# Lending dead SBUF as exponential buffers in a four-layer attention kernel, with fewer passes over the keys in its first layer

## The chip, the cores and the metric

The kernel runs as one launch on one core of a Trainium2 chip. The metric is the device time of the launch in microseconds; the profile is of one execution, and its times count from the first instruction.

## The reference

One sequence x of 2048 rows and 512 columns (bf16) goes through four layers with a residual each: A, B, A, B. Both A layers use the same weights, and so do both B layers.

```python
# A: 32 query heads of 16, one key and one value head for all of them
q = (x @ wq) as 32 heads;  k = x @ wk;  v = x @ wv
p = softmax(q k^T / 4)                  # 32 x 2048 x 2048
y = (p v) joined over the heads @ wo
# B: linear attention, 32 heads of 16
q, k, v = split(x @ wqkv);  phi(t) = where(t > 0, t + 1, exp(t)) + 1e-6
kv = sum_s phi(k)^T v;  z = sum_s phi(k)
y = (phi(q) kv / (phi(q) z + 1e-6)) joined @ wo
# each layer: x = x + layer(layernorm(x))
```

## The kernel before

**A planner writes the order.** The Python code does not emit instructions directly. It runs a small event simulation (class `Planner`): each operation (`op`) has a duration per engine, a latency, reads, writes and a priority; generators (`process`) wait for flags, for operations, or for a buffer from a pool (`acq`). The order in which the simulated engines take operations is written out per engine, with semaphore waits for the dependences. On the chip each engine runs its list in that fixed order, so durations in the code decide only the order. Operations that may run on ACT or DVE (`flex`, `copy_flex`) get the engine that is free first in the simulation.

**Softmax layers (L = 0 and 2, `run_a`).** x has 16 tiles of 128 rows. For a tile t the 32 heads are computed as two halves (`par`), each with four groups j of heads at four 32-row positions of PE. A *score block* is 128 keys x 512 (4 heads x 128 queries): 2 x 16 x 2 x 4 = 2048 blocks per layer, 4096 in all (`KM` and `QT`, L838). A *segment* (`Seg`) is one (t, par) with a range of key tiles `kts`; segments are computed in the order of `a_segs`. With all keys at once a tile has one segment per half. Early tiles run before all keys exist, in passes over ranges of keys:

```python
PASSES = ((0, 2), (2, 4))
LATE = ((4, 8), (8, 12), (12, 16))
```

The first four tiles take all of these, so that they have five segments each (tiles 2 and 3 have four).

**Two engines compute the exponentials.** Scores go to two sets of three PSUM banks. ACT takes a set's first two or all three banks with one exact exponential (L1006) into one of `NPT` = 6 buffers `PT`. Where DVE has time, it takes the third bank, or another free one (`dve_split`, `dve_open`, `alone`): it builds the exponential's bits with one addition and a maximum, written as int16 into a quarter of one of `NFB` = 12 buffers `FB` (L1085). Four such blocks make a chunk, and the chunk is copied three times with a fixed number added (a *shift*, L1127, `dve_shifts`); PE then multiplies all four versions with differently weighted values (`VW`), which smooths the error of the bit trick. So a block on ACT needs one product with V (L892, PT), a block on DVE four (L892, FB). Where PE has a gap, a filler matmul that adds zero is issued to keep its clock up (L937 in the softmax layers, L824 elsewhere).

**Sums.** A segment's products accumulate in one PSUM bank (`ACC`). At its end DVE copies the bank into a fp32 sum in `sacc` (L1150, first segment of a tile half) or adds it there (L1152). After the last one the sum is transposed, normalised and projected (`norm`, `epilogue`) and x is updated.

**Linear layers (L = 1 and 3, `run_b`)** are computed tile by tile as x tiles come out of the softmax layer before, in the gaps of the exponentials; phi uses one ACT activation (L1254) per 128x512. Their keys are accumulated over all tiles, so that the outputs of layer 1 wait for the last tile of layer 0; layer 2 starts as its x tiles come. Layer norm (`ln_tile`) writes `xn`, one of six buffers, and its transpose goes to `xnT` (512 x 2048, all 16 tiles), by a DMA transpose issued from SP or by PE.

**What starts the exponentials.** `act_stream` waits for the keys of tiles 0 and 1 and the first Q. Before a block is taken, all keys of its segment must be planned. DVE's exponentials start when the last key group is planned (`KGATE`). Thresholds for DVE's share: `BLS`, `BLT`, `BLO`, `DXB` (DVE's backlog in us up to which it takes a block), `FBO`, `FBS` (free FB buffers to keep), `AHEAD`, `CHT`, `ENDL` (how far ahead of ACT).

**Memory that is dead for a while.** `OB` and `OTB` (buffers of layer 1's output) are used by layer 1 alone; `wq` only while Q is computed; `wo2` (the weight of B) only at the end of each B layer; `xn` buffers little once the keys are done; `sacc` rows of early tiles after those tiles' end; and most of `xnT` after the queries of layer 2 are computed.

Of the kernel before, what the change touches and what calls it, by code (L numbers as in the profile page):

```python
# [6 lines left out]
BF16 = mybir.dt.bfloat16  # L7
# [28 lines left out]
class Planner:  # L36
# [39 lines left out]
    def op(self, opts, reads=(), writes=(), prio=5.0, lat=0.08, dma=False, name="", join=None, mode="full", port=False, after=()):  # L76
# [13 lines left out]
        for k in list(writes) + list(after):  # L90
            deps.update(self.ws(k))
            deps.update(self.readers.get(k, ()))
# [301 lines left out]
PASSES = ((0, 2), (2, 4))  # L394
LATE = ((4, 8), (8, 12), (12, 16))
# [22 lines left out]
PBL = 1.2  # L418


def bass_interleave_layers__grouped_kv_mqa__linear_attn_block__prompt_kernel(
# [66 lines left out]
    OB = sb("OB", [P, NOB, D], BF16)  # L488
    OTB = sb("OTB", [P, NOB, 4, P], BF16)
# [22 lines left out]
    def give(pool, item):  # L512
        if pool is banks and retire.get(item):
# [8 lines left out]
    pl.give = give  # L522

# [12 lines left out]
    def dma(dst, src, writes, prio, lat):  # L536
        return op({SP: (0.07, lambda e: e.dma_start(dst, src))}, writes=writes, prio=prio, lat=lat, dma=True)

    for t in range(4):
        dma(x_sb[:, t, :], xv[:, t, :], [("x", t)], 0.1 * t, 2.5 + 0.5 * t)  # L540
    dma(wk[:], A_wk.rearrange("(ft f) c -> f ft c", f=P), ["wk"], 1.0, 4.0)
    dma(wv[:], A_wv.rearrange("(ft f) c -> f ft c", f=P), ["wv"], 1.1, 4.2)
    dma(wq[:], A_wq.rearrange("(ft f) c -> f ft c", f=P), ["wq"], 1.2, 5.5)
    for b in range(1, 4):
        dma(x_sb[:, 4 * b:4 * b + 4, :], xv[:, 4 * b:4 * b + 4, :], [("x", t) for t in range(4 * b, 4 * b + 4)], 2.0 + 0.1 * b, 6.0 + 1.5 * b)
    def late():
# [3 lines left out]
        dma(wo2[:], B_wo.rearrange("(g r) c -> r g c", r=P), ["wo2"], 3.2, 16.0)  # L550
# [45 lines left out]
    def flex(fn_a, fn_d, da, dd, reads, writes, prio, aprio=None):  # L596
        return op({AC: (da, fn_a), DV: (dd, fn_d)}, reads=reads, writes=writes, prio=prio)

    def copy_flex(dst, src, reads, writes, prio, da=0.5, dd=0.62):
        return flex(lambda e: e.copy(dst, src), lambda e: e.tensor_copy(dst, src), da, dd, reads, writes, prio)  # L600
# [10 lines left out]
    xn_pool = Pool_(range(NXN))  # L611

    def dmat(dst, src, reads, writes, prio):
        return op({SP: (0.1, lambda e: e.dma_start(dst, src, transpose=True))}, reads=reads, writes=writes, prio=prio, lat=DTL, dma=True)
# [5 lines left out]
    def halves(bs, dst, key, prio, psrc=None):  # L620
        l = op({DV: (DH_DUR, lambda e: e.tensor_copy(dst(0), psrc(bs[0], 0)))}, writes=[B_(bs[0]), key], prio=prio)
        r = op({AC: (AH_DUR, lambda e: e.copy(dst(1), psrc(bs[1], 1)))}, writes=[B_(bs[1]), key], prio=prio, join=l)
# [53 lines left out]
    def ln_tile(t, prio, far=False, crit=False):  # L676
# [3 lines left out]
        else:  # L680
# [10 lines left out]
           reads=[("x", t), ("mv", t), ("rs", t)], writes=[("xn", i)], prio=prio, port=True)  # L691
        if far:
            o = dmat(xnT[:, :, t * P:(t + 1) * P], xn[:, i, :], [("xn", i)], [("xnT", t)], prio)
# [3 lines left out]
        if crit:  # L697
# [3 lines left out]
            halves(bs, lambda h: xnT[:, 2 * h:2 * h + 2, t * P:(t + 1) * P], ("xnT", t), prio, lambda b, h: bank_bf(b)[:, 0:2, :])  # L701
# [12 lines left out]
        c = copy_flex(xnT[:, :, t * P:(t + 1) * P], v, [], [B_(b), ("xnT", t)], prio, 0.48, 0.34)  # L714
        pl.give_after(banks, b, [c])


    def a_tile(L, t, prio):
# [5 lines left out]
        yield from ln_tile(t, prio, t >= FARA[L // 2], cr)  # L724
# [67 lines left out]
    def a_segs():  # L792
        segs = []
        done = 0
        for lo, hi in PASSES:
            for t in range(hi):
                kts = list(range(lo, hi)) if t < lo else list(range(hi))
                for par in range(2):
                    segs.append(Seg(len(segs), t, par, kts, t >= lo, False, 2 * t + par))
            done = hi  # L800
        for lo, hi in LATE:
            for t in range(done):
                for par in range(2):
                    segs.append(Seg(len(segs), t, par, list(range(lo, hi)), False, hi == T, 2 * t + par))
        for t in range(done, T):
            for par in range(2):
                segs.append(Seg(len(segs), t, par, list(range(T)), True, True, 0))
        return segs

    pt_pool = Pool_(range(NPT))  # L810
    fb_pool = Pool_(range(NFB))
# [17 lines left out]
    def run_a(L):  # L829
        segs = a_segs()  # L830
# [113 lines left out]
        def act_stream():  # L944
            yield ("flag", ("K", L, 0))
            yield ("flag", ("K", L, 1))
# [5 lines left out]
            while True:  # L952
# [3 lines left out]
                while len(group) < size[s_] and split is None and state["si"] < len(segs):  # L956
                    sg = segs[state["si"]]
                    if not sg.left:
                        state["si"] += 1
                        continue  # L960
# [6 lines left out]
                    while any(("K", L, kt) not in pl.flags for kt in sg.kts) or ("Q", L, sg.t) not in pl.flags:  # L967
# [725 lines left out]
```

## Time and profile before

| what | value |
|---|---|
| median of 3 runs | 1533.74 us |
| lowest, highest | 1529.07, 1533.83 us |
| span of the profiled execution | 1530.0 us (no other time is given for it) |
| first to last exponential of ACT, layer 0 | 13.41 to 730.53 us |
| step from layer 0's to layer 2's exponentials | 730.53 to 754.79 us |
| first to last exponential of ACT, layer 2 | 754.79 to 1492.30 us |
| tail | 1492.30 to 1530.00 us |
| busy: PE, DVE, ACT, POOL | 94%, 94%, 97%, 4% of the span |

A row of a group reads: line, engine, operation, output tile <- input tiles, shapes, count | busy time in us, mean ns of one | idle time of the engine just before them, and what ended it. Busy time counts overlapping instructions once; the mean is of each by itself, so the mean times the count can be more. A row of the busy table reads: stretch, its length, busy us of PE, PEld, DVE, ACT, POOL with instruction counts, the granted PE clock as a share of full speed, the DMA share and GB/s. A row of a timeline reads: start, length, engine, line, operation, output <- input, count, and in brackets idle time before it. Equal neighbours in a timeline are merged into one row with their count.

### The profile page before, as it was taken

What the parts mean: (1) busy time and instruction counts of PE and PEld (TensorE: products, weight loads), DVE (VectorE), ACT (ScalarE), POOL (GpSimd) and SP (SyncE); (2) the same over time, 40 slices, a digit from 0 to 9 for tenths busy, and PEclk for the clock granted to TensorE, in tenths of its full rate; (3) what the DMA queues carried; (4) which work ended last, traced back from release to release, by engine and by line L of the source; (5) the groups of instructions that cost most, each with busy time, mean ns of one, the idle gap of its engine ahead of it and who ended that gap; (6) DMA issues with size and microseconds to landing.
All of it is one profiled execution on the core that took longest, in us unless ns stands there. A gap on an engine that the chain in (4) does not pass through costs nothing.

```text
span 1530.0 us, 35778 instructions
## 1 busy us (share of the span) xinstructions
PE 1440.2 (94%) x14498; PEld 522.9 (34%) x14606; DVE 1440.2 (94%) x2702; ACT 1482.6 (97%) x1503; POOL 63.8 (4%) x126
## 2 busy tenths in 40 slices
PE   8999999999999999999999989999999999999998
PEld 4422222333332223333644323323333332333335
DVE  7999999999999999999767899999999999999996
ACT  7999999999999999999699999999999999999996
POOL 4000000000000000000011000000000000000001
PEclk8999999999999999999999999999999999999999
DMA  4100010000000000000000000100000000000001
GB/s 112 70 2 1 9 22 5 8 7 6 8 8 8 5 8 5 1 1 2 2 1 1 2 1 9 22 5 9 9 5 8 9 8 5 8 5 1 1 2 56
DMA packets 40434, 17.53 MB, mean 11 GB/s; under 512 B 34128, under 2 KB 39760, under 8 KB 40272
## 3 DMA queue, kind: packets, MB, share of 16 engines
q1 hardware_dynamic: 40272, 15.25, 4.3%
q8 instruction: 117, 1.92, 0.5%
q14 instruction: 45, 0.37, 0.1%
HBM read 5.28 MB, written 2.10 MB: 5 GB/s over the span
## 4 chain that ended last, share of the span: by engine, by line
PE 29%; DVE 25%; issue 22%; ACT 22%; POOL 1%; DMA 0%; SPq 0%; ACTq 0%; POOLq 0%
ACT PT L1006 21%; DVE FB L1085 12%; PE ps L892 11%; DVE FB L1127 9%; PE ps L838 8%; PE ps L606 3%; PE ps L763 2%; PE ps L937 2%; PE ps L1169 1%; DVE sacc L1150 1%; ACT phE L1254 1%; DVE sacc L1152 0%; DVE Osb L1180 0%; PE ps L824 0%; POOL rs L686 0%
## 5 line engine op out<-in xcount | busy, mean ns | idle before, releaser
L1006 ACT ACTIVATE PT<-ps 128x1024 bf16<-128x1024 f32 (+1 forms) x1342 | 1418.1, 1204 | 14.8 <-PE ps L838 7.4
L1085 DVE TENSOR_SCALAR FB<-ps 128x512 int16<-128x512 f32 x1022 | 672.7, 682 | 19.0 <-PE ps L838 17.0
L838 PE MATMUL ps<-QT,KM 32*128 32x512 bf16 x4096 | 543.9, 386 | 43.1 <-ACT PT L1006 29.2
L892 PE MATMUL ps<-FB,VW 128*32 128x512 bf16 x4088 | 537.8, 385 | 20.1 <-ACT PT L1006 10.3
L892 PE MATMUL ps<-PT,V 128*32 128x512 bf16 x3074 | 523.7, 387 | 7.1 <-ACT PT L1006 5.4
L1127 DVE TENSOR_SCALAR FB<-FB 128x2048 int16<-128x2048 int16 (+1 forms) x768 | 503.1, 678 | 1.0
L838 PEld LDWEIGHTS ps<-QT,KM 32*128 32x128 bf16 x4096 | 136.4, 91 | 437.4 <-ACT PT L1006 295.4
L892 PEld LDWEIGHTS ps<-FB,VW 128*32 128x32 bf16 x4088 | 136.2, 94 | 217.7 <-issue 110.2
L892 PEld LDWEIGHTS ps<-PT,V 128*32 128x32 bf16 x3074 | 128.5, 94 | 112.9 <-issue 61.5
L937 PE MATMUL ps<-QT,V 128*32 128x512 bf16 (+6 forms) x579 | 139.8, 315 | 0.9 <-DVE FB L1085 0.3
L686 POOL TENSOR_TENSOR rs<-ve,mhalf 128x1 f32<-128x1 f32 x64 | 43.4, 680 | 1394.9 <-DVE ve L684 1392.3
L606 PE MATMUL ps<-wqkv,xnT 128*128 128x512 bf16 (+1 forms) x212 | 66.5, 369 | 3.4 <-issue 2.1
L937 PEld LDWEIGHTS ps<-QT,V 128*32 128x32 bf16 x579 | 46.1, 95 | 62.8 <-issue 43.6
L1150 DVE COPY sacc<-ps 128x512 f32<-128x512 f32 x64 | 43.6, 681 | 10.1 <-PE ps L892 9.9
L1254 ACT ACTIVATE phE<-ps 128x512 bf16<-128x512 f32 (+1 forms) x66 | 41.4, 628 | 7.6 <-PE ps L763 6.2
L1169 PE MATMUL ps<-identF,sacc 128*128 128x128 f32 x256 | 46.0, 291 | 0.9 <-DVE sacc L1150 0.8
L682 DVE BATCH_NORM_STATS2 st<-x_sb 128x6 f32<-128x512 bf16 x60 | 40.7, 680 | 2.5 <-DMA x_sb<-in_A_x_dram 2.3
L1152 DVE TENSOR_TENSOR sacc<-sacc,ps 128x512 f32<-128x512 f32 x56 | 38.0, 678 | 1.8 <-PE ps L892 1.7
L763 PE MATMUL ps<-xnT,wqkv 128*128 128x128 bf16 x512 | 39.4, 220 | 0.1
L763 PE MATMUL ps<-xnT,wq 128*128 128x128 bf16 x480 | 38.6, 226 | 0.0
L606 PEld LDWEIGHTS ps<-wqkv,xnT 128*128 128x128 bf16 x272 | 22.1, 97 | 46.5 <-issue 34.6
L1169 PEld LDWEIGHTS ps<-identF,sacc 128*128 128x128 f32 x256 | 27.4, 140 | 20.7 <-issue 11.5
(142 smaller groups left out, 656.5 us busy)
## 6 DMA issues: line engine op xcount, KB each, us to landing
out_dram<-x_sb SPq DMA_DIRECT2D x16, 128.0 KB, 1.7
x_sb<-in_A_x_dram SPq DMA_DIRECT2D x3, 512.0 KB, 6.1
wqkv<-in_B_wqkv_dram SPq DMA_DIRECT2D x1, 1536.0 KB, 7.4
xnT<-xn SPq DMA_TRANSPOSE x36, 2.4
x_sb<-in_A_x_dram SPq DMA_DIRECT2D x4, 128.0 KB, 2.5
wq<-in_A_wq_dram SPq DMA_DIRECT2D x1, 512.0 KB, 4.2
wo<-in_A_wo_dram SPq DMA_DIRECT2D x1, 512.0 KB, 4.1
wo<-in_B_wo_dram SPq DMA_DIRECT2D x1, 512.0 KB, 8.3
```

The costliest lines, as they stand in the source:

```text
L606: return e.matmul(dst, lhsT=l, rhs=r, start=(k == 0), stop=(k == len(pairs) - 1))
L686: op({PO: (0.55, lambda e: e.tensor_tensor(out=rs[:, t:t + 1], in0=ve[:, t:t + 1], in1=mhalf[:], op=ALU.pow))}, reads=[("ve", t), "mhalf"] ...
L763: ins = e.matmul(dst[:, g * P:(g + 1) * P], lhsT=lhs(g, k), rhs=rhs(k), start=(k == 0), stop=(k == FT - 1))
L838: return e.matmul(bank(b), lhsT=KM[r, sg.par, kt * P:(kt + 1) * P], rhs=QT[r, sg.t, :], start=True, stop=True)
L892: ins = e.matmul(ps[32 * j:32 * j + 32, ACC * 512:(ACC + 1) * 512], lhsT=V[:, kt, :] if w is None else VW[:, kt, w, :], rhs=ap, start=(k = ...
L937: o = op({PE: (n / 2400.0, lambda e: e.matmul(ps[32 * j:32 * j + 32, b * 512:b * 512 + n], lhsT=V0[:], rhs=QT[:, sg.t, 0:n], start=st, sto ...
L1006: ex = op({AC: (0.051 + 0.4267 * n, lambda e, n=n, s_=s_, p_=p_: e.activation(PT[:, p_, 0:n * 512], ps[:, s_ * 512:(s_ + n) * 512], ACTF.E ...
L1085: o = op({DV: (0.602, lambda e: e.tensor_scalar(out=dst.bitcast(I16), in0=bank(b), scalar1=VB, scalar2=VLO, op0=ALU.add, op1=ALU.max))}, w ...
L1127: o = op({en: (du, lambda e, w=w, g_=g_: e.tensor_scalar(out=FB[:, g_, 0:n].bitcast(I16), in0=FB[:, f_, 0:n].bitcast(I16), scalar1=float(w ...
L1150: o = op({DV: (0.6, lambda e, src=src: e.tensor_copy(src, bank(ACC)))}, writes=[B_(ACC), key], prio=0.0, lat=0.15)
L1169: o = op({PE: (0.12, lambda e, c=c: e.transpose(ps[:, b * 512 + c * P:b * 512 + (c + 1) * P], src[:, c * P:(c + 1) * P], identF[:]))}, rea ...
L1254: op({AC: (0.07 + n / 1200.0, lambda e: e.activation(phE[:, i, 0:n], bank(b, n), ACTF.Exp))}, reads=[B_(b)], writes=[("phE", i)], prio=pr ...
```

## The change

Line numbers in the text are those of the kernel before.

- Layer 0's early tiles: two instead of four, with key ranges 0-2, 2-4 and 4-16. Layer 2: as before up to key tile 8, then 8-16 in one pass.
- In layer 0 the exponentials start with the first key tile, and a block waits only for its own key tile, not for all of its segment.
- Lent buffers ("guests"): two PT and two FB in the joined OB/OTB memory, four PT in xnT columns of tiles 4 to 15 (layer 2), one FB each in two rows of `sacc`, in four `xn` buffers, in `wq` and in `wo2`. `lend` puts a guest into its pool when its owner ("host") is done; `recall` takes it back near the end of the layer. The first write of a guest, and the first write of the host after it, get the dependences of the other (`behind`). FB buffers can so rise from 12 to as many as 18, PT from 6 to 8 in layer 0 and 10 in layer 2.
- `wq` is loaded a second time after layer 0, `wo2` after layer 0 (no longer at the start) and again after layer 2. Layer 3 uses only the first four tiles of xnT, in a ring.
- The planner's durations and latencies of loads are replaced by measured ones.
- Thresholds are set per softmax layer (`TUNE`).

```diff
-PASSES = ((0, 2), (2, 4))
-LATE = ((4, 8), (8, 12), (12, 16))
+SEQ = {0: ((2, 0, 2), (2, 2, 4), (2, 4, 16)), 2: ((2, 0, 2), (2, 2, 4), (4, 0, 4), (4, 4, 8), (4, 8, 16))}
...
+BACK = 2
+TUNE = {0: {"FBS": 5, "AHEAD": 15, "LAG": 0.15, "ENDL": 12, "FBO": 0, "BLO": 7.0, "DXB": 1.6, "BLT": 3.2},
+        2: {"FBS": 3, "DXB": 1.6, "ENDL": 9, "BLS": 1.0}}
...
-    OB = sb("OB", [P, NOB, D], BF16)
-    OTB = sb("OTB", [P, NOB, 4, P], BF16)
+    OBB = sb("OBB", [P, 2 * NOB, D], BF16)
+    OB = OBB[:, 0:NOB, :]
+    OTB = OBB[:, NOB:2 * NOB, :].rearrange("p n (g c) -> p n g c", c=P)
...
+    for i in range(2):
+        pts[NPT + i] = OBF[:, i * BUF:(i + 1) * BUF]
+        home["PT", NPT + i] = ob_keys
+        fbs[NFB + i] = OBF[:, i * 2048:(i + 1) * 2048]
+        home["FB", NFB + i] = ob_keys
+    for i in range(4):
+        pts[NPT + 2 + i] = xnT[:, i, 4 * P:S]
+        home["PT", NPT + 2 + i] = xt_keys
...
+    def recall(which):
+        for kind, i in which:
+            if (kind, i) not in lent:
+                continue
+            lent.discard((kind, i))
+            pool = pt_pool if kind == "PT" else fb_pool
+            if i in pool.free:
+                pool.free.remove(i)
+                returned(pool, i)
...
-    dma(wq[:], A_wq.rearrange("(ft f) c -> f ft c", f=P), ["wq"], 1.2, 5.5)
+    load_wq()
...
-        dma(wo2[:], B_wo.rearrange("(g r) c -> r g c", r=P), ["wo2"], 3.2, 16.0)
...
+    def ring(L, t):
+        return t % 4 if L == 3 else t
...
             yield ("flag", ("K", L, 0))
-            yield ("flag", ("K", L, 1))
+            globals().update(TUNE[L])
+            if L:
+                yield ("flag", ("K", L, 1))
...
-                    while any(("K", L, kt) not in pl.flags for kt in sg.kts) or ("Q", L, sg.t) not in pl.flags:
+                    while any(("K", L, kt) not in pl.flags for kt in (sg.kts if L else blk[:1])) or ("Q", L, sg.t) not in pl.flags:
...
-                ex = op({AC: (0.051 + 0.4267 * n, lambda e, n=n, s_=s_, p_=p_: e.activation(PT[:, p_, 0:n * 512], ps[:, s_ * 512:(s_ + n) * 512], ACTF.Exp, scale=EXPSC, bias=EXPBIAS))},
-                        writes=bk + [("PT", p_)], prio=1.0, lat=EX_LAT)
+                ex = op({AC: (0.051 + 0.4267 * n, lambda e, n=n, s_=s_, p_=p_: e.activation(pts[p_][:, 0:n * 512], ps[:, s_ * 512:(s_ + n) * 512], ACTF.Exp, scale=EXPSC, bias=EXPBIAS))},
+                        writes=bk + [("PT", p_)], prio=1.0, lat=EX_LAT, behind=guest(L, "PT", p_))
...
+        def spare():
+            if L == 0:
+                for i in range(2):
+                    lend(pt_pool, "PT", NPT + i)
+            yield ("flag", ("K", L, T - 1))
+            hold_xn()
+            if L == 0:
+                lend(fb_pool, "FB", NFB + 5)
+                for t in range(T):
+                    yield ("flag", ("Q", L, t))
+                lend(fb_pool, "FB", NFB + 4)
+                return
+            for t in range(T):
+                yield ("flag", ("x", 1, t))
+            lend(fb_pool, "FB", NFB + 5)
+            for i in range(2):
+                lend(fb_pool, "FB", NFB + i)
+            for t in range(T):
+                yield ("flag", ("Q", L, t))
+            lend(fb_pool, "FB", NFB + 4)
+            for i in range(4):
+                lend(pt_pool, "PT", NPT + 2 + i)
```

More of the change, by code (lines that the diff above doesn't have):

```diff
@@ L74, in ws, with op @@
         return self.writer.get(k, [])
-    def op(self, opts, reads=(), writes=(), prio=5.0, lat=0.08, dma=False, name="", join=None, mode="full", port=False, after=()):
+    def op(self, opts, reads=(), writes=(), prio=5.0, lat=0.08, dma=False, name="", join=None, mode="full", port=False, after=(), behind=()):
         o = Op()
@@ L89, in op @@
             deps.update(self.ws(k))
-        for k in list(writes) + list(after):
+        for k in list(writes) + list(after) + list(behind):
             deps.update(self.ws(k))
@@ L522, in bass_interleave_layers__grouped_kv_mqa__linear_attn_block__prompt_kernel, with lend, hold_xn, returned @@
     pl.give = give
+    pt_pool = Pool_(range(NPT))
+    fb_pool = Pool_(range(NFB))
+    xn_pool = Pool_(range(NXN))
+    xheld = {"on": False, "got": []}
+    def lend(pool, kind, i):
+        lent.add((kind, i))
+        plain_give(pool, i)
+    def hold_xn():
+        xheld["on"] = True
+        mine = [i for i in xn_pool.free if i >= 2]
+        xn_pool.free = [i for i in xn_pool.free if i < 2]
+        for i in mine:
+            give(xn_pool, i)
+    def returned(pool, item):
+        if pool is fb_pool and item == NFB + 3:
+            for i in xheld["got"]:
+                plain_give(xn_pool, i)
+            xheld["got"] = []
+        if pool is fb_pool and item == NFB + 4 and not seen & {"wq2"}:
+            seen.add("wq2")
+            load_wq(guests["wq"])
+        if pool is fb_pool and item == NFB + 5:
+            load_wo2(guests["wo2"])
+    def recall(which):
[7 more added lines that the diff above has]
+                returned(pool, i)
+    def load_wq(behind=()):
+        dma(wq[:], A_wq.rearrange("(ft f) c -> f ft c", f=P), ["wq"], 1.2, 3.7, 0.54, behind)
+    def load_wo2(behind=()):
+        dma(wo2[:], B_wo.rearrange("(g r) c -> r g c", r=P), ["wo2"], 3.2, 8.0, 0.54, behind)
     def claim(bs):
```

203 lines of the change are left out of this document (133 added, 70 removed).

## The prediction

> **What bounds the kernel now.** I read the page's busy times first, then the busy table over four stretches (the first softmax layer's exponentials, the step to the next softmax layer, its exponentials, the tail), then the groups by form, then the timelines of head and tail.
>
> ```profile
> span 1530.0 us, 35778 instructions
> PE 1440.2 (94%) x14498; PEld 522.9 (34%) x14606; DVE 1440.2 (94%) x2702; ACT 1482.6 (97%) x1503; POOL 63.8 (4%) x126
> PE 29%; DVE 25%; issue 22%; ACT 22%; POOL 1%; DMA 0%; SPq 0%; ACTq 0%; POOLq 0%
> ```
>
> ```profile
> core 0: us, PE busy (x) PEld busy (x) DVE busy (x) ACT busy (x) POOL busy (x), PEclk, DMA share, GB/s
> 13.41:730.53 717.12, 677.46 (x6748) 228.83 (x6794) 692.41 (x1266) 708.28 (x688) 25.06 (x41) 0.99 0.05 12
> 730.53:754.79 24.26, 24.25 (x341) 20.89 (x340) 20.42 (x63) 12.70 (x34) 2.34 (x5) 1.00 0.01 2
> 754.79:1492.30 737.51, 697.89 (x7039) 247.09 (x7094) 694.38 (x1294) 731.95 (x723) 24.67 (x44) 1.00 0.03 6
> 1492.30:1530.00 37.70, 32.94 (x289) 20.01 (x293) 24.98 (x46) 23.79 (x47) 4.03 (x4) 1.00 0.17 57
> ```
>
> In the two long stretches ACT idles 8.8 of 717.12 us and 5.6 of 737.51. So the time there is ACT's work: the exponentials that DVE does not take. DVE idles 24.7 and 43.1 us, not much more, and the chain runs through DVE (25%) as often as through ACT (22%). The two share one queue of 4096 score blocks (128x512 each), so the kernel is bound by both at once, ACT first.
>
> ```profile
> L1006 ACT ACTIVATE PT<-ps 128x1024 bf16<-128x1024 f32 x952 | 929.1, 1078 | 6.6 <-PE ps L838 3.1 <-PE ps L892 2.5
> L1085 DVE TENSOR_SCALAR FB<-ps 128x512 int16<-128x512 f32 x1022 | 672.7, 682 | 19.0 <-PE ps L838 17.0
> L1006 ACT ACTIVATE PT<-ps 128x1536 bf16<-128x1536 f32 x390 | 566.0, 1510 | 8.2 <-PE ps L838 4.3 <-PE ps L892 3.4
> L892 PE MATMUL ps<-FB,VW 128*32 128x512 bf16 x4088 | 537.8, 385 | 20.1 <-ACT PT L1006 10.3 <-DVE sacc L1150 4.1 <-DVE sacc L1152 2.2
> L1127 DVE TENSOR_SCALAR FB<-FB 128x2048 int16<-128x2048 int16 x762 | 500.0, 679 | 0.9
> L937 PE MATMUL ps<-QT,V 128*32 128x512 bf16 x213 | 71.6, 386 | 0.4 <-DVE FB L1085 0.3
> L1152 DVE TENSOR_TENSOR sacc<-sacc,ps 128x512 f32<-128x512 f32 x56 | 38.0, 678 | 1.8 <-PE ps L892 1.7
> ```
>
> ACT does 2 x 952 + 3 x 390 = 3074 blocks, DVE the other 1022. The mean durations overlap (the next instruction starts under the last one's end), so I take the step between starts from runs of one form, with the duration of the last taken off:
>
> ```profile
> 346.04 0.62 ACT L1254 ACTIVATE phE<-ps 128x512 bf16<-128x512 f32 x1
> 346.51 6.56 ACT L1006 ACTIVATE PT<-ps 128x1024 bf16<-128x1024 f32 x7
> 724.10 5.52 ACT L1006 ACTIVATE PT<-ps 128x1536 bf16<-128x1536 f32 x4
> L1006 ACT ACTIVATE PT<-ps x1342: 1018/1098/1767, 13.4 to 1490.6; 128x1024 bf16<-128x1024 f32 x141, 128x1536 bf16<-128x1536 f32 x51
> 911.61 1.28 DVE L1085 TENSOR_SCALAR FB<-ps 128x512 int16<-128x512 f32 x2
> 912.81 1.28 DVE L1127 TENSOR_SCALAR FB<-FB 128x2048 int16<-128x2048 int16 x2
> ```
>
> (6.56 - 1.10)/6 = 0.91 us for two blocks, (5.52 - 1.51)/3 = 1.34 for three, 346.51 - 346.04 = 0.47 for an activation of one block in the linear layer (phi); on DVE 1.28 - 0.68 = 0.60 for an exponential and for a shift over four of them; an addition lasts as long (678 ns) and is priced alike.
>
> **The change, part by part.** The counts of the changed kernel are read from its instruction order as built.
>
> *Exponentials.* ACT has 1008 of two blocks and 345 of three: 3051 blocks, so 23 move to DVE (14 in the first softmax layer, 9 in the second). First layer: +14 x 0.91 - 14 x 1.34 = -6.0 us. Second: +42 x 0.91 - 31 x 1.34 = -3.3.
>
> *Passes over the keys.* The additions into the fp32 sums fall from 56 to 28 (28 to 8 in the first layer). DVE: 23 exponentials and 21 more shifts cost 26.4 us, 28 additions give back 16.8: +9.6, of which roughly +3 in the first layer and +7 in the second. This fits under DVE's idle time if that shrinks: in the first layer from 24.7 to about 15. In the second it is tight:
>
> ```profile
> 200.00:300.00 100.00, 96.10 (x923) 30.18 (x931) 99.81 (x187) 98.96 (x101) 3.94 (x4) 1.00 0.05 11
> 800.00:850.00 50.00, 47.00 (x466) 20.66 (x472) 34.31 (x81) 50.00 (x46) 6.20 (x13) 1.00 0.01 1
> 1100.00:1200.00 100.00, 94.39 (x1014) 34.13 (x1019) 99.61 (x182) 99.46 (x104) 1.49 (x2) 1.00 0.04 8
> ```
>
> Of its 43.1 us idle, 15.7 lie at 800 to 850, before the last keys exist, and can't be used. The rest, 27.4, must take +7 and a stretch about 4 us shorter. Stretches with 0.2 to 0.4 idle in 100 exist, so it can be done; I take it as hidden.
>
> *PE.* 92 more products with shifted blocks, 23 fewer with ACT's: 69 at 537.8/4088 = 0.13 us are 9 us, which displace filler (L937; its widest form alone is 71.6). If a filler is not displaced they stand in front of the next scores: bound 0 to 9, I take 0, as filler is issued only into gaps.
>
> *Other ACT work.* In the second long stretch two activations for phi and one copy of that size go to the tail, 1.4 us, and key copies that change engines bring some 0.2 back: 3.3 saved becomes 4.5. The order between the two softmax layers is the same on PE, filler included: 24.26 stays.
>
> *Head.* The first scores wait only for their own key tile.
>
> ```profile
> 9.74 0.58 ACT L600 CAST QT<-ps 128x512 bf16<-128x512 f32 x1 [0.81 <-PE ps L763]
> 11.68 1.07 ACT L600 COPY xnT<-ps 128x512 bf16<-128x512 bf16 x2 [1.36 <-PE ps L709]
> 12.98 0.39 PE L838 MATMUL ps<-QT,KM 32*128 32x512 bf16 x2
> 13.41 1.02 ACT L1006 ACTIVATE PT<-ps 128x1024 bf16<-128x1024 f32 x1 [0.36 <-PE ps L838]
> 13.88 0.34 DVE L752 TENSOR_SCALAR KM<-ps,kmask 128x128 bf16<-128x128 f32 x1
> 14.99 2.37 ACT L1006 ACTIVATE PT<-ps 128x1024 bf16<-128x1024 f32 x2
> ```
>
> Q is there at 10.32; score to exponential takes 13.41 - 12.98 = 0.43; the first exponential comes at 10.8 instead of 13.41. Only two can run before key tile 1, which DVE wrote from 13.88 and ACT now writes between exponentials. I put the third at 14.4; before it stood at 14.99 + 0.91 = 15.9. So 1.5 us are won (0 if tile 1 comes later, 2.6 if it does not hold up the third), less 0.5 for one Q copy that ACT takes over: 1.0.
>
> *Tail.* ACT gets those three, 1.4 us:
>
> ```profile
> 1495.62 0.37 ACT L622 COPY OT<-ps 128x256 bf16<-128x256 bf16 x1 [3.32 <-PE ps L635]
> 1499.65 0.37 ACT L622 COPY xnT<-ps 128x256 bf16<-128x256 bf16 x1 [1.66 <-PE ps L635]
> ```
>
> The two gaps hold 5.0 us; I add 0.3 (0 to 1.4).
>
> *Lent memory.* wq and wo2 are loaded again. In the order the last reader of the lent wo2 stands 127 score blocks before the end of the first softmax layer, that of wq 103: at 717.12/2048 = 0.35 us, 44 and 36 us.
>
> ```profile
> wq<-in_A_wq_dram SPq DMA_DIRECT2D x1, 512.0 KB, 4.2
> wo<-in_B_wo_dram SPq DMA_DIRECT2D x1, 512.0 KB, 8.3
> ACT PT L1006 <- PE ps L892: 5.9, 17, 0.8
> ```
>
> Landing in 4.2 and 8.3 us, both are hidden; without that cover 8.3 us would fall into the step between the layers. On SP they wait behind the last transposes of the first layer, and only the second layer's stand behind them. As for more buffers by themselves: ACT waited for PV products, which free its buffers, for 5.9 us in 17 waits.
>
> The Trainium skill (Perfetto Trace Analysis, Identifying Performance Opportunities) says that a gap that keeps recurring on the engine that should be full can mean too few buffers. Here no such gap recurs; by that rule this part of the change would bring little, which the 5.9 us agree with.
>
> *Clock.*
>
> ```profile
> 20.00:40.00 20.00, 18.84 (x168) 7.96 (x167) 15.24 (x44) 17.67 (x16) 6.60 (x14) 0.74 0.34 71
> 40.00:60.00 20.00, 18.79 (x213) 8.37 (x213) 18.36 (x35) 20.00 (x22) 1.55 (x4) 1.00 0.32 119
> ```
>
> For part of 20 to 40 the granted clock was low (mean 0.74) and ACT lost 2.3 us against the next 20. The changed head has fewer warming matmuls before the first scores; the low stretch may go or double: -2.3 to +2.3, I take 0. The Trainium skill (TensorE: Matmul & The Clock Gate, Part 1) lets the clock drop after a window of some 3.4 us of idle PE. The trace differs: PE was 18.84 of 20 us busy. By the rule neither kernel would slow down here; the sum would be 2.3 lower.
>
> **Sum.** -6.0 - 4.5 - 1.0 + 0.3 = -11.2: a span of 1518.8. The profile gives its execution no time but the span, 1530.0; the runs' median, 1533.74, is 3.7 above it. Forecast: 1522.5 us. Its own range: head -1.6 to +1.0, clock 2.3 each way, tail up to +1.1, and DVE or PE giving back up to 4: 1517 to 1529.
>
> **Rivals.**
> 1. *DVE becomes the bound* (slower). If DVE cannot shed idle time, its 9.6 us come on top instead of ACT's going: 1533.74 + 9.6 - 1.0 = 1542. Against it: 24.7 and 27.4 us of idle that is not forced. For it: windows at 99.8% and 25% of the chain. It decides once ACT waits for the exponential that DVE shares a bank set with; ACT's idle in the long stretches would pass 20 us.
> 2. *No change.* The blocks shift, but waits of PE in its fixed order (scores behind the extra products) return the gain: 1533, by the head alone. For it: 9 us of PE work added where PE is 94% busy.
> 3. *Buffers do more.* They also remove ACT's idle before exponentials, 6.6 + 8.2 = 14.8 us: 1522.5 - 14.8 = 1508. For it: lent buffers let DVE run ahead. Against: only 5.9 of it was waiting for buffers.
> That the change does not do what it says is excluded by the order: 403 of ACT's exponentials write lent memory.
>
> **Chances.** Forecast 0.62, DVE bound 0.14, no change 0.12, buffers do more 0.12. A difference of 0.3% (4.6 us) is about what a measurement of this kernel can tell. Under 1529.1 lie nearly all of the forecast and the third rival: faster 0.74, same 0.13, slower 0.13. The range leaves out most of the first rival and half of the third: 1511 to 1535.
>
> **What would show it.** First exponential near 10.8; the two long stretches near 710 to 713 and 733; ACT idle in them still under 15 us; DVE idle near 15 and 31; 92 additions and copies at the sums in place of 120; step and tail within 1 us of 24.3 and 37.7. Wrong, if DVE's idle stays and ACT's grows, or if a reload ends the wait of a matmul between the layers.

## The result, and the profile after

The changed kernel takes 1508.74 us (median of 4 runs, 1507.14 to 1511.17) against 1531.56 for the kernel before (4 runs, one more than in the table of before): a ratio of 0.9856, 95% interval 0.9839 to 0.9874. It is 22.8 us faster, where 11.2 were forecast: the time lies 2.3 us below the range (1511 to 1535). The profiled execution took 1508.96 us, 1.8 more than its span.

The head of the page of the changed kernel: span, busy times, and the shares of the chain that ended last.

```profile
span 1507.2 us, 35873 instructions
PE 1420.5 (94%) x14512; PEld 515.1 (34%) x14630; DVE 1438.6 (95%) x2714; ACT 1470.6 (98%) x1515; POOL 67.9 (5%) x126
issue 46%; DVE 21%; PE 16%; ACT 15%; POOL 1%; DMA 0%; SPq 0%; POOLq 0%; ACTq 0%; DVEq 0%
```

ACT and DVE are still full, with 12.0 and 1.6 us less busy time in a span that is 22.8 us shorter. In the chain of work that ended last, "issue" (an engine waits for nothing that the profile shows) has 46%, where it had 22%.

Busy time of each engine over the same four stretches (first softmax layer, step, second softmax layer, tail); the columns are those of the prediction's first windows.

```profile
11.61:715.70 704.09, 663.33 (x6774) 224.58 (x6826) 692.65 (x1279) 700.98 (x692) 25.98 (x42) 1.00 0.06 13
715.70:740.35 24.65, 24.64 (x346) 21.27 (x344) 20.16 (x62) 13.00 (x32) 2.18 (x4) 1.00 0.01 2
740.35:1469.63 729.28, 693.81 (x7062) 245.16 (x7121) 692.73 (x1295) 726.49 (x731) 29.14 (x44) 1.00 0.03 7
1469.63:1507.20 37.57, 33.54 (x295) 20.27 (x296) 27.14 (x52) 25.46 (x50) 4.02 (x4) 1.00 0.17 57
```

The first exponential comes 1.8 us earlier, the first stretch is 13.0 shorter, the step 0.4 longer, the second stretch 8.2 shorter, the tail 0.1 shorter. ACT's idle time falls from 8.8 and 5.6 us to 3.1 and 2.8, DVE's from 24.7 and 43.1 to 11.4 and 36.6.

ACT's exponentials by form; the tile names now include the lent memory.

```profile
L1109 ACT ACTIVATE PT<-ps 128x1024 bf16<-128x1024 f32 x700 | 712.6, 1089 | 3.5 <-PE ps L933 2.5 <-PE ps L987 0.5
L1109 ACT ACTIVATE PT<-ps 128x1536 bf16<-128x1536 f32 x250 | 373.3, 1521 | 0.2
L1109 ACT ACTIVATE xnT<-ps 128x1024 bf16<-128x1024 f32 x187 | 195.6, 1083 | 0.2
L1109 ACT ACTIVATE OBB<-ps 128x1024 bf16<-128x1024 f32 x121 | 129.7, 1087 | 0.3
L1109 ACT ACTIVATE xnT<-ps 128x1536 bf16<-128x1536 f32 x51 | 75.2, 1499 | 0.2 <-PE ps L987 0.2
L1109 ACT ACTIVATE OBB<-ps 128x1536 bf16<-128x1536 f32 x44 | 66.1, 1509 | 0.0
```

They are 700 + 187 + 121 = 1008 of two blocks and 250 + 51 + 44 = 345 of three, as read from the order. The idle time before them is 4.4 us, where it was 14.8. Waits for products (L987), the sign of a buffer not yet read, have all but gone.

Where the 22.8 us came from, by ACT. Back to back, at the prediction's steps of 0.91 and 1.34 us, the exponentials take 1388.9 us before and 1379.6 after: -9.3. The two long stretches together went from 1454.6 to 1433.4; what they hold besides went from 65.7 to 53.8: -11.9. With the start (-1.8) and the step and tail (+0.3) that is all of it. This second term is called the rest below: ACT's waits, and its other work (51 phi activations in these stretches before and 49 after, and copies).

### The profile page after: what moved, and what is told of

Same layout as the page of the kernel before. It is cut to its first block, busy times and chain, and to the rows that moved or that the text cites. A ratio compares the mean times of both kernels' runs of the same rounds, so it can differ in the third digit from the quotient of the medians.

```text
span 1507.2 us, 35873 instructions
## 1 busy us (share of the span) xinstructions
PE 1420.5 (94%) x14512; PEld 515.1 (34%) x14630; DVE 1438.6 (95%) x2714; ACT 1470.6 (98%) x1515; POOL 67.9 (5%) x126
## 4 chain that ended last, share of the span: by engine, by line
issue 46%; DVE 21%; PE 16%; ACT 15%; POOL 1%; DMA 0%; SPq 0%; POOLq 0%; ACTq 0%; DVEq 0%
ACT PT L1109 12%; DVE FB L1190 8%; DVE FB L1232 5%; PE ps L987 5%; PE ps L933 4%; ACT OBB L1109 3%; PE ps L705 2%; PE ps L866 2%; POOL rs L789 1%; DVE xn L1190 1%; PE ps L1032 1%; DVE sacc L1190 1%; PE ps L1309 1%; DVE sacc L1289 1%; DVE wq L1232 1%
## 5 line engine op out<-in xcount | busy, mean ns | idle before, releaser
L1109 ACT ACTIVATE PT<-ps 128x1024 bf16<-128x1024 f32 (+1 forms) x950 | 1033.5, 1203 | 3.7 <-PE ps L933 2.5
L987 PE MATMUL ps<-FB,VW 128*32 128x512 bf16 x3020 | 497.7, 385 | 13.5 <-ACT PT L1109 6.1
L1190 DVE TENSOR_SCALAR FB<-ps 128x512 int16<-128x512 f32 x693 | 462.1, 687 | 1.7 <-PE ps L933 0.5
L987 PE MATMUL ps<-PT,V 128*32 128x512 bf16 x2150 | 442.7, 386 | 4.5 <-ACT PT L1109 2.8
L1109 ACT ACTIVATE xnT<-ps 128x1024 bf16<-128x1024 f32 (+1 forms) x238 | 266.6, 1172 | 0.5 <-PE ps L987 0.2
L1232 DVE TENSOR_SCALAR FB<-FB 128x2048 int16<-128x2048 int16 x394 | 263.5, 683 | 0.1
L1109 ACT ACTIVATE OBB<-ps 128x1024 bf16<-128x1024 f32 (+1 forms) x165 | 193.6, 1200 | 0.3
L987 PEld LDWEIGHTS ps<-FB,VW 128*32 128x32 bf16 x3020 | 122.1, 94 | 153.6 <-issue 78.9
L987 PE MATMUL ps<-xnT,V 128*32 128x512 bf16 x527 | 140.8, 385 | 0.6 <-ACT PT L1109 0.2
L987 PEld LDWEIGHTS ps<-PT,V 128*32 128x32 bf16 x2150 | 107.1, 94 | 72.5 <-issue 41.3
L987 PE MATMUL ps<-OBB,V 128*32 128x512 bf16 x374 | 108.2, 386 | 1.1 <-ACT PT L1109 0.6
L987 PE MATMUL ps<-xn,VW 128*32 128x512 bf16 x248 | 69.8, 384 | 2.4 <-ACT OBB L1109 1.0
L987 PE MATMUL ps<-wo,VW 128*32 128x512 bf16 x232 | 69.2, 386 | 1.1 <-ACT OBB L1109 0.5
L987 PE MATMUL ps<-wq,VW 128*32 128x512 bf16 x228 | 67.7, 386 | 1.1 <-ACT xnT L1109 0.5
L987 PE MATMUL ps<-sacc,VW 128*32 128x512 bf16 x232 | 64.2, 385 | 1.4 <-DVE sacc L1289 0.8
```

Source lines behind the costliest of these rows:

```text
L987: ins = e.matmul(ps[32 * j:32 * j + 32, ACC * 512:(ACC + 1) * 512], lhsT=V[:, kt, :] if w is None else VW[:, kt, w, :], rhs=ap, start=(k = ...
L1109: ex = op({AC: (0.051 + 0.4267 * n, lambda e, n=n, s_=s_, p_=p_: e.activation(pts[p_][:, 0:n * 512], ps[:, s_ * 512:(s_ + n) * 512], ACTF. ...
L1190: o = op({DV: (0.602, lambda e: e.tensor_scalar(out=dst.bitcast(I16), in0=bank(b), scalar1=VB, scalar2=VLO, op0=ALU.add, op1=ALU.max))}, w ...
L1232: o = op({en: (du, lambda e, w=w, g_=g_: e.tensor_scalar(out=fbs[g_][:, 0:n].bitcast(I16), in0=fbs[f_][:, 0:n].bitcast(I16), scalar1=float ...
```

## The experiments

Line names below are those of each kernel's own code: the line of the exponentials, of the scores and of the products shifts by a few lines from run to run. "Weight" is what ACT's exponentials weigh against those of before (difference in number of each form times 0.91 and 1.34 us); "rest" is the time's change less the weight; it is taken from the whole time, so that it holds the start, the step and the tail too (-13.5 for the changed kernel, where the two long stretches give -11.9). Each change of time is against the runs of before on the same chip.

| kernel | time, us | change | weight | rest | ratio (95%) |
|---|---|---|---|---|---|
| changed | 1508.74 | -22.8 | -9.3 | -13.5 | 0.9856 (0.9839 to 0.9874) |
| no lending | 1532.69 | +2.2 | -13.9 | +16.1 | 1.0015 (1.0005 to 1.0025) |
| only FB lent | 1523.87 | -7.1 | -16.6 | +9.5 | 0.9959 (0.9944 to 0.9973) |
| only PT lent | 1528.25 | -2.7 | -7.4 | +4.7 | 0.9985 (0.9976 to 0.9995) |
| old passes | 1520.91 | -9.6 | -6.6 | -3.0 | 0.9941 (0.9925 to 0.9956) |
| old thresholds | 1520.13 | -10.3 | -7.5 | -2.8 | 0.9933 (0.9915 to 0.995) |
| old head and loads | 1509.89 | -21.1 | -11.6 | -9.5 | 0.987 (0.9855 to 0.9885) |
| lending alone | 1522.63 | -7.8 | -5.2 | -2.6 | 0.9947 (0.993 to 0.9963) |
| passes alone | 1533.36 | +1.9 | -6.7 | +8.6 | 1.0018 (1.0008 to 1.0027) |
| thresholds alone | 1538.47 | +7.5 | -12.7 | +20.2 | 1.0058 (1.0043 to 1.0073) |
| one threshold back | 1515.70 | -15.8 | -10.4 | -5.4 | 0.9895 (0.9875 to 0.9916) |
| other thresholds | 1506.16 | -25.3 | -11.5 | -13.8 | 0.9835 (0.9819 to 0.9852) |
| old passes, thin additions | 1521.52 | -10.0 | -6.6 | -3.4 | 0.9938 (0.9919 to 0.9956) |
| order of no lending, spare buffers | 1532.99 | +0.5 | -13.9 | +14.4 | 0.9999 (0.9985 to 1.0012) |
| order of before, spare buffers | 1531.32 | -1.2 | 0.0 | -1.2 | 0.9992 (0.998 to 1.0004) |

The weight, which the prediction priced, lies between -5 and -17 us in every kernel that gives DVE more to do, and says nothing about which of them is fast. The rest runs from +20 to -14 and decides.

### One part taken out at a time

**No lending.** No guest enters a pool; wo2 is loaded at the start again.

```diff
     def lend(pool, kind, i):
+        if kind not in LEND:       # LEND = ()
+            return
         lent.add((kind, i))
         plain_give(pool, i)
```

> The changed kernel with no buffer lent (6 PT and 12 FB throughout, wo2 loaded once at the start, xnT without the ring); passes, thresholds, head and load times as changed. Theory 1, the lent buffers took the waits of ACT and DVE away: at least half of the gain of about 23 us is lost, 1520 us or more. Theory 2, the fewer passes did it, and theory 3, the thresholds did it: 1514 or less. By ACT's count alone (0.91 and 1.34 us per exponential) it does 4.5 us less than the changed kernel, which would give 1504.

1532.69 us: the whole gain is gone, although ACT does 4.6 us less exponential work than in the changed kernel. Its groups and ACT's waits (us, times, longest) show where it went:

```profile
L1116 ACT ACTIVATE PT<-ps 128x1024 bf16<-128x1024 f32 x978 | 950.5, 1065 | 17.1 <-PE ps L994 12.9 <-PE ps L940 3.0
L1116 ACT ACTIVATE PT<-ps 128x1536 bf16<-128x1536 f32 x362 | 523.5, 1484 | 5.2 <-PE ps L994 3.7 <-PE ps L940 0.7
```

```profile
ACT PT L1116 <- PE ps L994: 16.6, 20, 4.7
ACT PT L1116 <- PE ps L940: 3.7, 11, 0.5
```

L994 is the line of the products, L940 that of the scores. ACT idles 22.3 us before exponentials, 16.6 of it for products that free a buffer, in single waits of up to 4.7 us. These waits look like the price of a late buffer on the chip; the runs with spare buffers, below, show that they are not.

**Old passes.**

```diff
-SEQ = {0: ((2, 0, 2), (2, 2, 4), (2, 4, 16)), 2: ((2, 0, 2), (2, 2, 4), (4, 0, 4), (4, 4, 8), (4, 8, 16))}
+SEQ = dict.fromkeys((0, 2), ((2, 0, 2), (2, 2, 4), (4, 0, 4), (4, 4, 8), (4, 8, 12), (4, 12, 16)))
```

> The changed kernel with the key ranges of before in both softmax layers (56 additions instead of 28), all else as changed. Theory 2, each segment end stops PE and DVE for longer than its addition: 1520 or more. Theories 1 and 3: only the additions come back, 28 x 0.60 = 16.8 us on DVE, which is 16 blocks at 1.05 us, shared by two engines that do 3.15 blocks per us: 5 us, so 1512 to 1515.

1520.91: the passes are worth some 12 us beside the rest of the change, not the 5 of the additions and not nothing. The time is the one that theory 2 named.

**Old thresholds.**

```diff
-TUNE = {0: {"FBS": 5, "AHEAD": 15, "LAG": 0.15, "ENDL": 12, "FBO": 0, "BLO": 7.0, "DXB": 1.6, "BLT": 3.2},
-        2: {"FBS": 3, "DXB": 1.6, "ENDL": 9, "BLS": 1.0}}
+TUNE = {0: {}, 2: {}}
```

> The changed kernel with the thresholds of before in both softmax layers, all else as changed. Theory 3, DVE's queue limits filled its idle time: 1520 or more. Theories 1 and 2: 1512 or less.

1520.13: 11 us, of which the exponentials' weight is 1.8. The time is the one that theory 3 named, but its mechanism, that the limits filled DVE's idle time, is not what the gain is made of: ACT's blocks rise only from 3051 to 3056. So each of the three theories has its own number come true, each part taken out costs 11 us or more, and these three runs do not decide between them.

**Old head and loads.** The exponentials wait for the keys of the whole segment again, and the planner has its old times for loads.

```diff
-            if L:
-                yield ("flag", ("K", L, 1))
+            yield ("flag", ("K", L, 1))
...
-    dma(wk[:], A_wk.rearrange("(ft f) c -> f ft c", f=P), ["wk"], 1.0, 2.05, 0.46)
+    dma(wk[:], A_wk.rearrange("(ft f) c -> f ft c", f=P), ["wk"], 1.0, 4.0)
```

> The changed kernel with the old start of the exponentials (whole segment's keys awaited) and the old planned load times. Count alone (one fewer of each ACT form in the first layer) -2.3 us, prediction's head +1.0: 1507.5. Rival 1, the start matters through the clock: the low-clock stretch at 20 to 40 us is back and ACT waits some 2.8 us more there: 1511 to 1512, with the granted clock under 0.9 in that window. Rival 2, the traced load times place the work of the whole order better: 1515 or more.

1509.89 (1509.11 to 1511.90), which overlaps the runs of the changed kernel (1507.14 to 1511.17). These two parts are worth nothing that can be measured.

### One part alone

**Lending alone** (old passes, thresholds, head and loads: the edits above, and nothing of the change but the guests).

> The kernel before with the lent buffers alone (passes, thresholds, head and load times of before). Theory 1: most of the gain, 1520 or less. Theories 2 and 3: within 4 us of before, 1527 to 1535. By ACT's count it does 5.3 us less than before, which would give 1526.

1522.63: -7.8, two thirds of it weight and one third rest. It lies between what theory 1 and theories 2 and 3 had named. The two long stretches of this kernel, then those with old passes and with old thresholds:

```profile
13.61:718.63 705.02, 667.81 (x6725) 223.28 (x6771) 695.74 (x1278) 702.90 (x690) 26.54 (x41) 1.00 0.06 13
744.44:1481.10 736.66, 701.47 (x7056) 247.40 (x7114) 694.03 (x1291) 731.24 (x735) 31.13 (x44) 1.00 0.03 6
```

```profile
10.43:723.85 713.42, 667.32 (x6804) 226.21 (x6852) 703.94 (x1303) 702.23 (x690) 27.41 (x42) 1.00 0.06 13
748.13:1480.21 732.08, 696.25 (x7042) 245.45 (x7099) 693.60 (x1300) 729.39 (x727) 28.10 (x44) 1.00 0.03 7
```

```profile
10.75:715.45 704.70, 665.53 (x6788) 225.50 (x6838) 693.67 (x1280) 700.76 (x691) 27.95 (x42) 1.00 0.06 13
739.89:1477.86 737.97, 699.37 (x7088) 246.53 (x7147) 690.56 (x1290) 732.68 (x732) 30.97 (x44) 1.00 0.03 6
```

Against 717.12 and 737.51 before, and 704.09 and 729.28 after: in the first softmax layer lending alone brings 12.1 us (2.3 of it is the clock of the profiled execution of before, see the last section), and the two kernels with old thresholds are as short there as the changed one. With new thresholds and old passes the layer takes 8.4 us more than with both old (it starts 3.2 earlier and ends 5.2 later): the new thresholds cost there unless the passes go with them. In the second layer lending alone brings 0.9, and both kernels with new thresholds are short (732.08 and 729.28). So what the thresholds bring depends on the passes and on the layer: no part has a price of its own.

**Passes alone.**

> The kernel before with only the fewer passes (no lending, old thresholds, old head and load times). Interaction theory (without the lent buffers the order can't use DVE's freed time): 1528 to 1534, ACT's wait for PV products at or above 5.9 us. By counts (3 more of two and 6 fewer of three blocks in the first layer, 3 fewer and 1 more in the second: -6.7 us): 1524. As much as they bring beside lending: 1519.

1533.36: no gain, as the interaction theory had it (ACT waits 7.6 us for products, 5.9 before); the 12 us that the passes bring beside lending are not there.

**Thresholds alone.**

> The kernel before with only the new planner thresholds (no lending, old passes, old head and load times). Interaction theory (the thresholds ask for more buffers than there are): no gain or a loss, 1530 to 1542, with ACT's wait for PV products above the 5.9 us of before. Rival (the thresholds help by themselves, as the 11 us they bring beside lending): 1519. Count alone (20 more of two and 21 fewer of three in the first layer, 19 more and 15 fewer in the second: -12.7 us): 1518.

1538.47: 7.5 us slower, though 12.7 us of ACT's exponentials are gone. ACT's largest sum of waits is the one for products, 5.9 us before:

```profile
ACT PT L1113 <- PE ps L994: 19.6, 27, 2.1
```

### Which of the lent buffers

Both are the changed kernel with `LEND = ("FB",)` or `LEND = ("PT",)` in the edit of the run without lending.

> The changed kernel with only the FB guests lent (DVE's exponentials); PT stays at its own 6 buffers. Which kind of lent buffer carries the gain? FB theory: the gain stays, 1505 to 1512. PT theory: ACT's waits for PV products come back as without lending (16.6 us of 'ACT PT <- PE' there), 1525 to 1533. By the count of ACT's exponentials alone (11 more of two and 10 fewer of three blocks in the first layer, 19 fewer and 10 more in the second: -7.3 us) 1501.

> The changed kernel with only the PT guests lent (ACT's exponentials: 2 more in layer 0, 4 more in layer 2); FB stays at 12. PT theory: the gain stays, 1508 to 1513, and ACT does not wait for PV products. FB theory: 1525 to 1533, DVE's idle before exponentials is back near 14 us. Count alone (+2 us of ACT exponentials against the changed kernel): 1511.

1523.87 and 1528.25: FB alone keeps 8.8 of the 24 us between no lending and all of it, PT alone 4.4; both theories of one kind fall, though the FB theory had the run with PT alone right (1525 to 1533, and DVE's idle before exponentials back at 12.9 us). Together they bring 10.7 more than the sum.

### Engine time or order

**Thin additions.** Old passes, and each of the 56 additions into the fp32 sums now handles 32 of its 512 columns; the planner keeps its price, so the order stays.

```diff
-o = op({DV: (0.6, lambda e, src=src: e.tensor_tensor(out=src, in0=src, in1=bank(ACC), op=ALU.add))},
+o = op({DV: (0.6, lambda e, src=src: e.tensor_tensor(out=src[:, 0:32], in0=src[:, 0:32], in1=bank(ACC)[:, 0:32], op=ALU.add))},
```

> The kernel with the old passes (everything else changed), its order kept to the last instruction, but each of the 56 additions into the fp32 sums adds only 32 of its 512 columns: some 28 us of DVE's time go, the planned order stays. Leaves out: most of the additions. Engine theory (the additions matter because they take DVE's time, and ACT then waits for what DVE does late): the 12 us that the passes brought come back with no change of order, 1508 to 1513. Order theory (the passes matter because the planner made another order from them): the freed time becomes idle time of DVE, 1517 to 1521.

1521.52, against 1520.91 with whole additions: no gain, and 0.5 us above what the order theory named. DVE takes the same operations in the same order in both profiles. The additions' own busy time falls by 28 us, and DVE's in all by 20 (1448.4 to 1428.5):

```profile
L1292 DVE TENSOR_TENSOR sacc<-sacc,ps 128x512 f32<-128x512 f32 x56 | 38.3, 683 | 1.9 <-PE ps L987 1.8
```

```profile
L1292 DVE TENSOR_TENSOR sacc<-sacc,ps 128x32 f32<-128x32 f32 x56 | 10.1, 180 | 3.3 <-PE ps L987 2.9
```

Additions that take 28 us less on a 95% busy engine bring nothing. PE's waits for them go as well, from 7.2 to 1.1 us, and bring nothing either. In this order, fixed beforehand, the work that disappears becomes idle time. So the passes do not pay through the additions, and the passes alone, where the planner made an order from them without lending, brought no gain: that they pay through the order made of them together with the rest follows from these two runs. One piece is left open: with old passes PE also waits 5.5 us at the copies into the sums, and 1.6 in the changed kernel; the thin additions leave those waits as they are (5.2).

**One threshold back**, FBS in the first softmax layer:

```diff
-TUNE = {0: {"FBS": 5, "AHEAD": 15,
+TUNE = {0: {"FBS": 4, "AHEAD": 15,
```

> The changed kernel with one threshold put back, FBS 5 to 4 in the first softmax layer. ACT's exponentials weigh the same (491 and 173 in place of 480 and 181 in the first layer, 507 and 178 in place of 528 and 164 in the second: -0.7 and -0.4 us). If the time follows the counts: 1507 to 1509. If it hangs on how well the whole order fits, so that any one threshold can cost as much as a part of the change: 1512 to 1516, all of it in ACT's waits.

1515.70 (1513.06 to 1517.06): 7 us slower than the changed kernel, 4 to 7 if only executions at a mean clock of 1.000 are taken, with 1.1 us less exponential work. In the profiles ACT's idle time grows by 6.8 us of the span's 7.8, part of it the low clock of this one (mean 0.997). One step of one number costs about half as much as a whole part. This suggests that the thresholds' 11 us are the gain of a search over orders and not of a rule; it is not shown.

**Other thresholds.**

```diff
+TUNE = {0: {"FBS": 5, "AHEAD": 12, "LAG": 0.15, "ENDL": 6, "FBO": 0, "BLO": 6, "BLS": 1.8, "BLT": 3.2, "DXB": 1.4},
+        2: {"FBS": 3, "AHEAD": 20, "LAG": 0.1, "ENDL": 9, "FBO": 0, "BLO": 9, "BLS": 1.0, "BLT": 3.2, "DXB": 1.4}}
```

> The changed kernel with other thresholds in both softmax layers, found by trying some 580 sets in the planner. ACT's exponentials weigh 1.3 us less in the first layer and 0.7 less in the second. If ACT's waits stay: 1505 to 1508. If the fit of the order is as fragile as the one threshold says, anything up to 1513.

1506.16 (1506.08 to 1506.40): the fastest of all, 0.9835 of before, and inside what was named for the case that ACT's waits stay. Its interval overlaps that of the changed kernel, so the 2.6 us between them are likely, not shown.

### The same order with more buffers

What was left: do the buffers act on the chip, or through the planner? The pools get the guests, but count them as spare: no more are in use at a time in the plan than without lending, so the planner makes the old order, and each buffer is reused later than it was. The profiles agree: ACT, DVE and POOL run the same operations on the same shapes in the same order as in the kernel with fewer buffers.

```diff
+    def left(self):
+        return len(self.free) - self.spare
...
-                if pool.free and not pool.wait:
+                if pool.left() > 0 and not pool.wait:
...
         lent.add((kind, i))
+        pool.spare += 1
         plain_give(pool, i)
```

> The order of the run without lending, instruction by instruction on PE, ACT, DVE and POOL, but written into as many buffers as the changed kernel has: a lent buffer goes into the ring, while no more of them are in use at a time in the plan than before, so each is reused later than it was. Only SP's loads of wq and wo2 differ. Chip theory (an exponential waits on the chip for its buffer to be read; 16.6 us of ACT's waits for PV products without lending): these waits go, 1512 to 1518. Order theory (the buffers act through the planner, which makes another order when it has more of them): the waits stay or move to the scores, 1529 to 1533.

> The order of the kernel before on PE, ACT, DVE and POOL, with the lent buffers as spares in its ring. Chip theory: its 5.9 us of waits for PV products go, and with them perhaps the waits too short to show as idle time: 1519 to 1526. Order theory: 1529 to 1532.

1532.99 and 1531.32: +0.5 us against before (+2.2 for the same order with fewer buffers) and -1.2. By the medians neither order gains more than 2 us from the buffers; the intervals leave at most some 6 us in the first and 3 in the second, far from 24. Both times are those of the order theory. ACT's waits in the order of no lending:

```profile
ACT PT L1117 <- PE ps L941: 12.5, 23, 4.3
...
ACT OBB L1117 <- PE ps L941: 2.2, 3, 1.7
```

The wait for products, 16.6 us with the longest at 4.7, has gone but for 0.9, and one for scores (L941) of 12.5 + 2.2 with the longest at 4.3 stands in its place. The longest wait without the spare buffers, and with them:

```profile
514.63 1.94 ACT L1116 ACTIVATE PT<-ps 128x1024 bf16<-128x1024 f32 x2 [4.71 <-PE ps L994]
```

```profile
516.83 1.02 ACT L1117 ACTIVATE PT<-ps 128x1024 bf16<-128x1024 f32 x1 [4.32 <-PE ps L941]
```

Counted along ACT's list, the second stands exactly one instruction later than the first, and the next two (2.10 and 2.02 us, now 1.72 and 1.62) have moved by one as well. The spare buffer lets ACT run one exponential further; then the scores of the next one are missing, which stand behind the same products in PE's order, and ACT waits nearly as long. The buffer was only what was late last. In the first of these waits PE's list has nine filler matmuls (L1039), so the planner had already planned a gap there; that it did so for want of a buffer is likely, not shown. In the order of before, the 7.4 us for scores and 5.9 for products became these, 10.1 in place of 13.3:

```profile
ACT PT L1113 <- PE ps L940: 6.9, 20, 0.9
...
ACT xnT L1113 <- PE ps L940: 2.0, 6, 0.5
...
ACT OBB L1113 <- PE ps L940: 1.2, 4, 0.4
```

This shows the way: the lent buffers are worth their 24 us to the planner, and nothing that can be measured to an order made without them. What in the better order does it, which instruction stands where, was not isolated.

## Why the prediction was wrong

- **Exponentials: right.** -9.3 us by count and step; the trace has the counts, and the steps fit.
- **The failed step is the rest.** The sum let ACT's waits stand ("ACT idle in them still under 15 us") and had no term for more buffers, as only the 5.9 us of waits for products stood against them. It had none for the thresholds, and for the passes none beyond DVE's time for the additions. The two long stretches came at 704.1 and 729.3 us, where 710 to 713 and 733 were named. The rest fell by 11.9 us in the profiles. The forecast for it was -1.2 (other ACT work moved to the tail). That is 10.7 of the span's miss of 11.6 us (2.3 of them the clock of the execution that was profiled before); the start holds most of what is left. What the runs show in its place: taken out of the changed kernel, the lending costs 24 us, the passes 12 and the thresholds 11, where the count of exponentials gives -4.6, +2.7 and +1.8. The mistake was one of kind: with an order planned beforehand a shortage of buffers has already been turned into order when the trace is taken. The waits that the trace shows are not the price of the shortage, and the run with spare buffers shows that even those were not worth their 5.9 us (1.2 came).
- **The rule on buffers.** The Trainium skill (Perfetto Trace Analysis, Identifying Performance Opportunities) names a recurring gap as a sign of too few buffers; by it this part would bring little. For the chip the runs agree: buffers alone, in the order of before, brought 1.2 us, inside the error. A planner that makes the order from the number of buffers is another case, and there going by the gap misled.
- **The third rival** had the time (1508) and the quantity that goes (14.8 us of idle before exponentials; 10.4 went). Its mechanism, DVE running ahead on more buffers, is not shown; the spare buffers show that without a new order nothing of it comes. That its time fits so well is in part luck: its span would be 1518.8 - 14.8 = 1504.0, and 1507.2 was measured; the error in going from span to median (below) covers 1.9 of this. It was given 0.12 because of the 5.9 us: the argument that failed.
- **The first and second rivals** did not come about in the whole, but the order without lending is the second rival nearly as written: blocks shift, waits return the gain. Thresholds alone are slower, through waits that the first rival's price did not contain.
- **DVE's added work as hidden: right.** Its idle time fell to 11.4 and 36.6 us where 15 and 31 were named. The 92 additions and copies at the sums came as well (28 and 64).
- **Head: half right.** The first exponential came at 11.61, not 10.8, the third at 16.43, where 14.4 was named and 15.9 stood before:

```profile
11.61 1.94 ACT L1109 ACTIVATE PT<-ps 128x1024 bf16<-128x1024 f32 x2 [0.70 <-PE ps L933]
...
15.28 0.77 ACT L854 ACTIVATE KM<-ps,kmask 128x128 bf16<-128x128 f32 x2 [0.89 <-PE ps L705]
16.43 4.62 ACT L1109 ACTIVATE PT<-ps 128x1024 bf16<-128x1024 f32 x4 [0.38 <-PE ps L933]
```

  ACT's idle stretch before key tile 1 is what the prediction allowed for as "0 if tile 1 comes later". The run with the old head, slower by 1.2 us with runs that overlap, cannot tell the worth of the head from zero.
- **Step, tail and reloads: right** (24.65 and 37.57 for 24.3 and 38.0). The reloads land in 4.1 us and lengthen no stretch:

```profile
wq<-in_A_wq_dram SPq DMA_DIRECT2D x2, 512.0 KB, 4.1
wo<-in_B_wo_dram SPq DMA_DIRECT2D x2, 512.0 KB, 4.0
```

- **Span to median: wrong by 1.9 us.** The prediction took 3.7, the profiled span against the median of three runs. In nearly every run the time is 1.7 to 2.2 us above its own span (2.8 at most); the median belonged to another execution than the profile. The forecast's own range is not the sum of its terms either: these give 1518.6 to 1530.9, not 1517 to 1529.
- **Clock: the term was zero.** 2.3 us of the difference between the two profiles are the clock, not the change (below). The medians hold executions at both clocks, so they too can hold 1 or 2 us of it; the executions at a full clock, given below, are at least 19.7 us apart.

## What to carry over

Where a planner fixes the order beforehand, price a resource that it plans with (buffers, thresholds, its own durations) by what another order could save, up to all of the waits and overlap still missing, and not by the waits for that resource in the old trace. Counting moved work from the new order gives the direction and a part of the size; here the part that no count shows ran from +20 to -14 us. And do not add up the parts of such a change: the passes alone and the thresholds alone were slower than before (by 1.9 and 7.5 us), and lending alone brought a third of the gain.

## What the hardware showed that was not expected

**A low clock in some executions of nearly every kernel.** The stretch at 20 to 40 us with a granted clock of 0.74 before is absent in the changed kernel's profile, and present in that of the run with thin additions, whose head is the changed one:

```profile
20.00:40.00 20.00, 17.77 (x199) 8.51 (x200) 17.64 (x54) 20.00 (x19) 7.95 (x17) 1.00 0.41 70
```

```profile
20.00:40.00 20.00, 17.96 (x164) 8.16 (x166) 15.08 (x49) 17.78 (x18) 7.95 (x17) 0.77 0.42 77
```

ACT is busy 20.00 us in the one and 17.78 in the other. The mean clock of whole executions tells the same: of the kernel before, runs at 1.000 took 1528.7 to 1532.2 us, those at 0.994 to 0.997 took 1531.7 to 1536.6; the changed kernel took 1507.1 to 1509.0 at 1.000 and 1511.17 at 0.996. It is a matter of the execution, worth 2 to 4 us by these times, and a single profile of each kernel can differ by it. The Trainium skill's rule quoted in the prediction (TensorE: Matmul & The Clock Gate, Part 1) would tie it to idle PE. PE was busy 17.96 of these 20 us at the low clock and 17.77 at the full one. In the first 45 us of all three profiles, those of before, after and thin additions, no gap between PE's matmuls is longer than 0.7 us. What sets the low clock off was not tried.

**Recorded durations cover waits.** An exponential of two blocks is recorded with 1078 ns on average, while back to back one starts every 0.91 us. An engine whose next instruction is late by less than that overlap still shows as busy. Of the rest that went, 11.9 us, ACT's idle time shows only 14.4 - 5.9 = 8.5. Most of the other 3.4 lies under the exponentials' own records: their busy time fell by 12.1 us (1418.1 to 1406.0), where the steps give 9.3.
